# Five weight tiles of the second MoE are kept with a stationary operand's words 2, 4, 6, 8 and 12 words apart

## The chip, the cores and the metric

The kernel runs on one core of a Trainium2 chip. The metric is the device time of one execution in microseconds (us), the median of several runs. One execution was also recorded by the hardware profiler; every row below comes from that record.

## The reference

Inputs are q, k, v and a complex decay per channel (batch 4, 8 heads, 768 steps, 48 channels). A linear-attention recurrence gives 3072 tokens of 384 values, and two feed-forward blocks follow:

```python
x = attn_out.transpose(0, 2, 1, 3).reshape(3072, 384)
h = x @ w_in                                   # 384 -> 2048
x = (h * np.clip(h + 3, 0, 6) / 6) @ w_out     # 2048 -> 384
a, b = x @ w1, x @ w2                          # 384 -> 1024 each
out = ((a * b) @ w3) @ w_out2                  # 1024 -> 1024 -> 384
```

All weights arrive as float64 and are turned into float32 on the chip.

## The kernel before

Precision. A weight or activation is split into a high word (fp32r, rounded by a ScalarE copy) and a low word (fp32r, what VectorE's subtraction leaves). A product of two split operands is three matmuls: high by high, high by low, low by high (`mm3`, L742 to L744). Each matmul has its own stationary load of 128 columns on 128 partitions.

Stages. Until about 586 us attention and the first MoE run interleaved. Then w3 and w_out2 are folded into one 1024x384 matrix (`fold`, L1041 to L1043, up to 620 us). From 620 us to the end the second MoE runs: six blocks of 512 tokens (`two`), and in each block eight slices i of 128 hidden channels. For a slice, `b1` makes x @ w1 and then x @ w2: nine matmuls each (three 128-row pieces kk of the 384 inputs, three products each), with the weight as the stationary operand and 512 tokens as the moving one. ScalarE copies the first result out of PSUM, VectorE multiplies it with the second, and the product is split into `gh` and `gl`. Two slices later `b2` multiplies it with the folded matrix: four token groups of three matmuls, `gh` or `gl` stationary and 384 columns moving (L1104 to L1106).

Weight tiles. Slice i uses columns from group g = i // 2 of w1 and w2: tiles ("1", g) and ("2", g), each 128 partitions by 384 x 256 / 128 = 768 words. A tile is loaded and turned into float32 by `decode` and split by `split` (L764 to L770) into a buffer w of shape [128, 2, 768], tag "W": 768 high words, then 768 low words, each ordered (kk, half i, column). So the 128 words of one stationary operand lie side by side. Three of the eight tiles, ("1", 0), ("2", 0) and ("1", 1), are split elsewhere (`PLACES`) into freed buffers of other names (`ar`, `Kc`, `k`, `q`, `Ks`, `xf`); the other five live in "W". In the profile the second MoE's matmuls and loads named `x<-W` with no second name are just these five; those with a second name are the other three.

Order. A planner (`Plan`) writes the order of each engine's instructions in advance, from estimated durations and due times. Buffers of one tag are handed on when their last reader is done.

Of the kernel before, what the change touches and what calls it, by code (L numbers as in the profile page):

```python
# [7 lines left out]
F32 = mybir.dt.float32  # L8
# [5 lines left out]
AF = mybir.ActivationFunctionType  # L14
ALU = mybir.AluOpType
# [9 lines left out]
EXP_SET, TRIG_SET = "natural_log_exp_and_others", "trig_and_small"  # L25

PLACES = {("o", 0): ("u", "u"), ("o", 1): ("u", "cs"), ("o", 2): ("s1", "s1"), ("o", 3): ("ai", "ai"), ("1", 0): ("ar", "Kc"), ("2", 0): ("k", "q"), ("1", 1): ("Ks", "xf")}
BUFS = {'u': 3, 'ai': 2, 's1': 2, 'ce': 1}


# [226 lines left out]
def c_act(n, psum=False):  # L257
    return n / 1200.0 + (0.05 if psum else 0.095)


def c_tt(n):
    return n / 960.0 + 0.07
# [10 lines left out]
def c_mm(n):  # L273
    return n / 2308.0 + 0.009
# [145 lines left out]
def main_kernel(tc, q, k, v, a_re, a_im, w_in, w_out, w1, w2, w3, w_out2, consts, qT, kT, arT, aiT, vT, wiT, woT, w1T, w2T, w3T, wo2T, out, blocks=(2, 2, 4, 4, 4, 4, 4)):  # L420
# [8 lines left out]
    KD, KF, KI = DM // 128, DFF // 128, DF2 // 128  # L429
# [15 lines left out]
    with tc.tile_pool(name="keep", bufs=1) as kp:  # L445
      c5_ = kp.tile([128, 2, 128], F32, name="c2")
      flag = kp.tile([1, 1], I32, name="flag")
      with ctx:
# [4 lines left out]
        def SB(tag, shape, n=1, dt=F32, free=0, key=None):  # L453
            return P.buf(tag, lambda: sb.tile(shape, dt, tag=tag, name=tag, bufs=P.slots[tag]), n, free, key)

        def WB(shape):

            return SB("W", [128, 2] + shape, NW, F32R)

        def part(w, i, shape):  # L460
            return w()[:, i].rearrange("p (a b) -> p a b", a=shape[0])

        def PS(tag, shape, n=1, free=0):
            return P.buf("ps" + tag, lambda: ps.tile(shape, F32, tag=tag, name=tag, bufs=P.slots["ps" + tag]), n, free)
# [28 lines left out]
        def ACT(dur, fn, r, w, **kw):  # L493
            return P.add("ACT", dur, fn, r, w, **kw)

        def DVE(dur, fn, r, w, **kw):
            return P.add("DVE", dur, fn, r, w, **kw)

        def PE(dur, fn, r, w, **kw):
            return P.add("PE", dur, fn, r, w, **kw)  # L500
# [4 lines left out]
        def A(o, i, f, scale=1.0, bias=0.0, **kw):  # L505
            act.activation(out=o, in_=i, func=f, scale=scale, bias=bias, **kw)  # L506

        def TT(o, i0, i1, op):
            dve.tensor_tensor(out=o, in0=i0, in1=i1, op=op)  # L509
# [10 lines left out]
        def cut(t_, shape):  # L520

            if list(t_.shape) == list(shape):
                return t_
            names = "abc"[:len(shape) - 1]
            size = 1
            for x in shape[1:]:
                size *= x
            s_ = " ".join(names)
            return t_.rearrange("p %s -> p (%s)" % (s_, s_))[:, :size].rearrange("p (%s) -> p %s" % (s_, s_), **dict(zip(names, shape[1:])))
# [13 lines left out]
        def group(gi):  # L543
# [7 lines left out]
            def nb(name, shape=None, n=1, tag=None, full=None):  # L551
                shape = shape or [128, KD, w]
                full = full or shape[:-1] + [shape[-1] * GT // C] if name != "ys" else [128, 4, GT, 128]
                tag = tag or name
                return P.buf(tag, lambda: cut(sb.tile(full, F32, tag=tag, name=tag, bufs=P.slots[tag]), shape), BUFS.get(tag, n))
            ar, ai, kk, qq = (nb(x) for x in ("ar", "ai", "k", "q"))
# [111 lines left out]
        def chunk(u, c_, Kc, KT, QT, ys, mt):  # L668
# [4 lines left out]
            def nb(name, shape=None, n=1, tag=None):  # L673
                return SB(tag or name, shape, BUFS.get(tag or name, n))
            vb = vt[u % 2]
# [65 lines left out]
        def mm3(o, wh, wl, xh, xl, start, stop, **kw):  # L741
            pe.matmul(o, wh, xh, start=start, stop=False, **kw)  # L742
            pe.matmul(o, wh, xl, start=False, stop=False, **kw)  # L743
            pe.matmul(o, wl, xh, start=False, stop=stop, **kw)  # L744

        def load64(src, shape, free, after=()):

            n = shape[0] * shape[1]
            raw = SB("W", [128, 768], NW, U64, free, "raw")
            DMA(lambda e_: e_.dma_start(out=raw()[:, :n].rearrange("p (a b) -> p a b", a=shape[0]), in_=src), after, [raw], n * 1024)  # L750
            return raw, lambda i: raw()[:, :n].bitcast(I32).rearrange("p (n two) -> p n two", two=2)[:, :, i]
# [10 lines left out]
            DVE(c_tt(n), lambda: dve.scalar_tensor_tensor(out=ov().bitcast(I32), in0=words(1), scalar=-0x80000000, in1=words(0), op0=ALU.bitwise_and, op1=ALU.bitwise_or), [lo_], [dst])  # L762
            return lo_

        def split(raw, f):

            w = WB([768])
            ACT(c_act(768), lambda: A(w()[:, 0], f(), AF.Copy), [raw], [w])
            DVE(c_tt(768), lambda: TT(w()[:, 1], f(), w()[:, 0].bitcast(F32), ALU.subtract), [raw, w], [w], part=True)
            return w  # L770

        def packed(raw, n):
            return lambda: raw()[:, :n].bitcast(F32).rearrange("p (two n) -> p two n", two=2)[:, 0, :]

        def pieces(src, i):
            a = KD if src is not woT and src is not wo2T else 2
            return src[i].rearrange("p (a b) -> p a b", a=a), (a, 768 // a)
# [5 lines left out]
        def decode(src, i, after=()):  # L783
            n_ = len(taken_up)
            after = list(after) + ([ready0] if n_ >= EARLY else []) + ([taken_up[n_ - AHEAD]] if n_ >= AHEAD else [])
            src, shape = pieces(src, i)
            raw, words = load64(src, shape, 2, after)
            f = packed(raw, 768)
            taken_up.append(to32(raw, words, 768, raw, f, n_ in EASED))
            return raw, shape  # L790
# [158 lines left out]
        for js in [range(FIRST)] + [[j] for j in range(FIRST, len(blk))]:  # L949
# [18 lines left out]
            for j in js:  # L968
                n = blk[j][1]
# [5 lines left out]
        def half(w, p, i):  # L975

            bufs, shape = w
            if type(bufs) is list:
                t_ = bufs[i]()[:, p]
                return t_.rearrange("p (a b) -> p a b", a=KD) if shape[0] == KD else t_  # L980
            t_ = part(bufs, p, shape)
            return t_[:, :, i * 128:i * 128 + 128] if shape[0] == KD else t_[:, i]

        def of(w, i):
            return w[0][i] if type(w[0]) is list else w[0]

        def later(nm, src, g):
            tags = PLACES.get((nm, g))
            after = [seen[23]]
            if tags is None:  # L990
                raw, shape = decode(src, g, after)
                return split(raw, packed(raw, 768)), shape
            src, shape = pieces(src, g)
            raw, words = load64(src, shape, 1, after)
            f = packed(raw, 768)
            to32(raw, words, 768, raw, f)
            ws = []
            for i, tag in enumerate(tags):
                w = SB(tag, [128, 2, 384], 1, F32R)
                fv = lambda i=i: (f().rearrange("p (a b) -> p a b", a=KD)[:, :, i * 128:i * 128 + 128] if shape[0] == KD else f()[:, i * DM:i * DM + DM])  # L1000
                wv = lambda j, w=w: (w()[:, j].rearrange("p (a b) -> p a b", a=KD) if shape[0] == KD else w()[:, j])
                ACT(c_act(384), lambda fv=fv, wv=wv: A(wv(0), fv(), AF.Copy), [raw], [w])
                DVE(c_tt(384), lambda fv=fv, wv=wv: TT(wv(1), fv(), wv(0).bitcast(F32), ALU.subtract), [raw, w], [w], part=True)
                ws.append(w)
            return ws, shape
# [68 lines left out]
        def b1(j, i, xs):  # L1074
            n = two[j][1] * 128
            pr = []
            for nm in ("1", "2"):
                p_ = PS("x", [128, 512], 5)
                w = wq[nm, i // 2]

                def mm(p_=p_, w=w):
                    wh, wl = half(w, 0, i % 2), half(w, 1, i % 2)
                    for kk in range(KD):
                        mm3(p_()[:, :n], wh[:, kk], wl[:, kk], xs[kk]()[:, 0, :n], xs[kk]()[:, 1, :n], kk == 0, kk == KD - 1)
                PE(9 * c_mm(n), mm, [of(w, i % 2)] + list(xs), [p_, bseq], pin=pins["a", j, i])
                pr.append(p_)
            c = i % 3
            a = SB("r", [128, 512], 2)
            ACT(c_act(n, True), lambda: A(a()[:, :n], pr[0]()[:, :n], AF.Copy), [pr[0]], [a], boost=MB)
            DVE(c_tt(n), lambda: TT(a()[:, :n], a()[:, :n], pr[1]()[:, :n], ALU.mult), [pr[1]], [a], boost=MB)  # L1090
            gh, gl = SB(("u", "u", "s1")[c], [128, 512], 2, F32R), SB(("ai", "ai", "s1")[c], [128, 512], 2, F32R)
            ACT(c_act(n), lambda: A(gh()[:, :n], a()[:, :n], AF.Copy), [a], [gh], boost=MB)
            DVE(c_tt(n), lambda: TT(gl()[:, :n], a()[:, :n], gh()[:, :n].bitcast(F32), ALU.subtract), [a, gh], [gl], boost=MB)
            return gh, gl
# [15 lines left out]
        for j, (a, n) in enumerate(two):  # L1110
            P.bias = -60
            xs = [SB("W", [128, 2, 512], NW, F32R, 2, "xs") for _ in range(KD)]
# [101 lines left out]
```

## Time and profile before

| | |
|---|---|
| median of 3 runs | 928.56 us (926.35 to 928.78) |
| the profiled execution | 927.13 us |
| its span, first to last instruction | 924.9 us |
| TensorE busy | 881.3 us, 95% |
| stationary loads (PEld) busy | 759.0 us, 82% |
| VectorE busy | 585.4 us, 63% |
| ScalarE busy | 508.8 us, 55% |

The span is what the instructions took; the 2.2 us beside it are start and end. Busy shares are averages over stages with different limits. Matmuls are pipelined, so a matmul's record is longer than the distance to the next one; the distance between starts is what it costs. Stationary loads are recorded apart (PEld) and overlap with the matmul before them.

### The profile page before, as it was taken

The page shows a single profiled execution, that of the slowest core. Times are in us where ns is not written, and L with a number is a line of the kernel's source. Part 1 is how long each engine was busy: PE and PEld are TensorE (multiplying, and loading weights), DVE is VectorE, ACT ScalarE, POOL GpSimd, SP SyncE. Part 2 cuts the span into 40 slices and gives each one's busy share as a digit, 9 for nine tenths or more (in the row PEclk, how much of TensorE's full clock was granted, in tenths as well). Part 3 has the DMA queues.
Part 4 walks back from the last instruction along what each step waited for, and adds up shares of the span by engine and source line. Part 5 has one row for each costly group of instructions (what it writes and reads, how often), then busy time and mean ns, then how long its engine had stood idle before and what let it go on. Part 6 is the DMA issues. An engine that isn't in the chain of part 4 may idle for free.

```text
span 924.9 us, 13311 instructions
## 1 busy us (share of the span) xinstructions
PE 881.3 (95%) x5194; PEld 759.0 (82%) x5194; DVE 585.4 (63%) x913; ACT 508.8 (55%) x816; POOL 0.2 (0%) x4
## 2 busy tenths in 40 slices
PE   0689999999999999999999999999999999999997
PEld 0478989888888888878888888998888888888886
DVE  6999999889998787869454699652223223222221
ACT  7999888978887567656423576442222222222221
POOL 0000000000000000000000000000000000000000
PEclk9999999999999999999999999999999999999999
DMA  7895736367581645365424666230100101010001
GB/s 266 213 238 168 198 109 168 95 130 173 157 203 47 165 132 149 80 146 170 94 47 131 195 238 235 93 94 21 34 35 7 62 1 46 1 35 0 16 20 38
DMA packets 55991, 102.88 MB, mean 111 GB/s; under 512 B 6384, under 2 KB 34160, under 8 KB 55920
## 3 DMA queue, kind: packets, MB, share of 16 engines
q1 hardware_dynamic: 55920, 101.94, 39.0%
q8 instruction: 43, 0.70, 0.3%
q14 instruction: 28, 0.23, 0.1%
HBM read 64.62 MB, written 13.63 MB: 85 GB/s over the span
## 4 chain that ended last, share of the span: by engine, by line
PE 75%; DVE 12%; ACT 8%; DMA 3%; issue 1%; SPq 1%; ACTq 0%; DVEq 0%
PE x L742 12%; PE x L743 12%; PE x L744 12%; PE m L742 5%; PE m L743 5%; PE m L744 5%; PE x L693 4%; PE m L1106 3%; PE m L1104 3%; PE m L1105 3%; ACT u L506 2%; ACT W L506 2%; PE x L705 2%; DVE gl L509 1%; PE x L710 1%
## 5 line engine op out<-in xcount | busy, mean ns | idle before, releaser
L506 ACT ACTIVATE r<-x 128x512 f32<-128x512 f32 (+1 forms) x144 | 82.2, 572 | 152.7 <-PE x L744 130.1
L509 DVE TENSOR_TENSOR r<-r,x 128x512 f32<-128x512 f32 x48 | 33.0, 688 | 178.8 <-PE x L744 178.8
L742 PE MATMUL m<-gh,W 128*128 128x512 f32 (+1 forms) x288 | 110.1, 382 | 0.5 <-ACT gh L506 0.5
L743 PE MATMUL m<-gl,W 128*128 128x512 f32 (+1 forms) x288 | 107.7, 374 | 0.9 <-DVE gl L509 0.7
L744 PE MATMUL m<-gh,W 128*128 128x512 f32 (+1 forms) x288 | 107.2, 372 | 0.0
L506 ACT ACTIVATE gh<-r 128x512 fp32r<-128x512 f32 (+1 forms) x96 | 56.7, 593 | 72.9 <-PE m L744 69.3
L742 PE MATMUL x<-xh,W 128*128 128x512 f32 x240 | 96.3, 401 | 0.0
L743 PE MATMUL x<-xl,W 128*128 128x512 f32 x240 | 93.7, 390 | 0.0
L744 PE MATMUL x<-xh,W 128*128 128x512 f32 x240 | 93.6, 390 | 0.0
L509 DVE TENSOR_TENSOR gl<-r,gh 128x512 fp32r<-128x512 f32 (+1 forms) x96 | 61.9, 645 | 43.9 <-ACT gh L506 42.5
L742 PE MATMUL x<-W 128*128 128x512 f32 (+1 forms) x228 | 84.5, 371 | 0.0
L744 PE MATMUL x<-W 128*128 128x512 f32 (+1 forms) x228 | 84.1, 369 | 0.0
L743 PE MATMUL x<-W 128*128 128x512 f32 (+1 forms) x228 | 84.0, 368 | 0.0
L880 DVE SCALAR_TENSOR_TENSOR r<-r,x 128x512 f32<-128x512 f32 (+1 forms) x96 | 61.2, 639 | 13.1 <-ACT r L506 12.7
L506 ACT ACTIVATE W<-W 128x768 f32<-128x768 f32 (+3 forms) x78 | 64.7, 852 | 5.3 <-DMA W<-in_w3T_dram 2.7
L743 PEld LDWEIGHTS m<-gl,W 128*128 128x128 f32 x288 | 54.2, 188 | 11.0 <-DVE gl L509 2.4
L742 PEld LDWEIGHTS m<-gh,W 128*128 128x128 f32 x288 | 54.2, 188 | 11.0 <-issue 0.9
L744 PEld LDWEIGHTS m<-gh,W 128*128 128x128 f32 x288 | 54.2, 188 | 9.6
L506 ACT ACTIVATE u<-r 128x512 fp32r<-128x512 f32 x36 | 22.7, 632 | 63.6 <-DVE r L509 63.6
L742 PEld LDWEIGHTS x<-xh,W 128*128 128x128 f32 x240 | 45.1, 188 | 10.2 <-issue 0.9
L744 PEld LDWEIGHTS x<-xh,W 128*128 128x128 f32 x240 | 45.0, 188 | 9.8
L743 PEld LDWEIGHTS x<-xl,W 128*128 128x128 f32 x240 | 45.1, 188 | 8.4
(216 smaller groups left out, 1911.3 us busy)
## 6 DMA issues: line engine op xcount, KB each, us to landing
KT<-Kc SPq DMA_DIRECT2D x72, 129.0 KB, 3.6
QT<-cs SPq DMA_DIRECT2D x72, 128.0 KB, 4.5
W<-in_w3T_dram SPq DMA_DIRECT2D x16, 512.0 KB, 4.4
v<-in_vT_dram SPq DMA_DIRECT2D x24, 256.0 KB, 2.7
W<-in_wiT_dram SPq DMA_DIRECT2D x8, 768.0 KB, 7.3
W<-in_woT_dram SPq DMA_DIRECT2D x8, 768.0 KB, 7.5
ar<-in_arT_dram SPq DMA_DIRECT2D x12, 384.0 KB, 3.4
ai<-in_aiT_dram SPq DMA_DIRECT2D x12, 384.0 KB, 3.4
```

Of the source, the lines that this page charges most:

```text
L506: act.activation(out=o, in_=i, func=f, scale=scale, bias=bias, **kw)
L509: dve.tensor_tensor(out=o, in0=i0, in1=i1, op=op)
L693: pe.matmul(p_()[:, i, :], KT()[:, 4 * g + i, tok], QT()[:, 4 * g + i, tok])
L705: pe.matmul(py()[64 * j:64 * j + 64, p, :], vb.ap[:, h, :], Pm[h // 4]()[:, h % 4, :], start=True, stop=first, tile_position=(0, 64 * j), ...
L710: pe.matmul(py()[64 * j:64 * j + 64, p, :], Ap.ap[:, h, :], QT()[:, h, tok], start=False, stop=True, tile_position=(0, 64 * j), skip_group ...
L742: pe.matmul(o, wh, xh, start=start, stop=False, **kw)
L743: pe.matmul(o, wh, xl, start=False, stop=False, **kw)
L744: pe.matmul(o, wl, xh, start=False, stop=stop, **kw)
L880: DVE(c_tt(n), lambda: dve.scalar_tensor_tensor(out=r()[:, :n], in0=r()[:, :n], scalar=6.0, in1=h()[:, :n], op0=ALU.min, op1=ALU.mult), [h ...
L1104: pe.matmul(o, gh()[:, a], Wb()[:, 0, i % 2], start=(i == 0), stop=False)
L1105: pe.matmul(o, gh()[:, a], Wb()[:, 1, i % 2], start=False, stop=False)
L1106: pe.matmul(o, gl()[:, a], Wb()[:, 0, i % 2], start=False, stop=(i == KI - 1))
```

## The change

The five tiles that live in "W" get other orders of their 1536 words. `LAID` names for each the distance between neighbouring words of one stationary operand (one kk, one half i, high or low): ("2", 1) 2 words, ("1", 2) 4, ("2", 2) 6, ("2", 3) 8 and ("1", 3) 12. For 2 words, high and low alternate; for 4, the halves i and high/low are interleaved; for 6, the three kk and the halves; for 12, all of these; for 8, kk 0 and 1 are interleaved with everything else, and kk 2 lies behind them with a distance of 4 words. `split` writes the same words with the same engines to the new places, in one instruction each, except that the tile with 8 words needs two on each engine (512 and 256 words). `half` hands `b1` the strided views. The values, the loads' number, the matmuls, the buffers and the planner's costs are as before.

```diff
+LAID = {("2", 1): 2, ("1", 2): 4, ("2", 2): 6, ("1", 3): 12, ("2", 3): 8}
-        def split(raw, f):
+        def split(raw, f, kind=None):
             w = WB([768])
-            ACT(c_act(768), lambda: A(w()[:, 0], f(), AF.Copy), [raw], [w])
-            DVE(c_tt(768), lambda: TT(w()[:, 1], f(), w()[:, 0].bitcast(F32), ALU.subtract), [raw, w], [w], part=True)
+            if kind is None:
...
+            src = lambda: f().rearrange("p (k i c) -> p k i c", k=KD, i=2)
+            def put(fn):
+                for k0, k1 in laid(w, kind, 0)[1]:
+                    fn(laid(w, kind, 0)[0](k0, k1), laid(w, kind, 1)[0](k0, k1), src()[:, k0:k1])
+            ACT(c_act(768), lambda: put(lambda h, l, x: A(h, x, AF.Copy)), [raw], [w])
+            DVE(c_tt(768), lambda: put(lambda h, l, x: TT(l, x, h.bitcast(F32), ALU.subtract)), [raw, w], [w], part=True)
             return w
+        def laid(w, kind, q):
+            x = lambda: w().rearrange("p a b -> p (a b)")
+            whole = ((0, KD),)
+            if kind == 2:
+                return lambda a, b: x().rearrange("p (k i c q) -> p q k i c", k=KD, i=2, q=2)[:, q, a:b], whole
+            if kind == 4:
+                return lambda a, b: x().rearrange("p (k c i q) -> p q k i c", k=KD, i=2, q=2)[:, q, a:b], whole
+            if kind == 6:
+                return lambda a, b: x().rearrange("p (q c k i) -> p q k i c", k=KD, i=2, q=2)[:, q, a:b], whole
+            if kind == 12:
+                return lambda a, b: x().rearrange("p (c k i q) -> p q k i c", k=KD, i=2, q=2)[:, q, a:b], whole
+            return lambda a, b: (x()[:, :1024].rearrange("p (c k i q) -> p q k i c", k=2, i=2, q=2)[:, q] if a == 0 else
+                                 x()[:, 1024:].rearrange("p (k c i q) -> p q k i c", k=1, i=2, q=2)[:, q]), ((0, 2), (2, 3))
...
+            if type(shape[0]) is tuple:
+                get, cuts = laid(bufs, shape[1], p)
+                return [get(a, b)[:, k, i] for a, b in cuts for k in range(b - a)]
...
-                return split(raw, packed(raw, 768)), shape
+                kind = LAID.get((nm, g))
+                return split(raw, packed(raw, 768), kind), (shape if kind is None else (shape, kind))
...
-                        mm3(p_()[:, :n], wh[:, kk], wl[:, kk], xs[kk]()[:, 0, :n], xs[kk]()[:, 1, :n], kk == 0, kk == KD - 1)
+                        mm3(p_()[:, :n], at_k(wh, kk), at_k(wl, kk), xs[kk]()[:, 0, :n], xs[kk]()[:, 1, :n], kk == 0, kk == KD - 1)
```

## Rows read from the trace of the kernel before

**Rows 1.** The page: the granted TensorE clock in 40 slices.
```profile
PEclk9999999999999999999999999999999999999999
```

**Rows 2.** The chain that ended last, 620 to 924.9 us, shares by line.
```profile
by line: PE x L743 21.7%; PE x L744 21.7%; PE x L742 21.5%; PE m L1106 8.3%; PE m L1104 8.3%; PE m L1105 8.3%; PE x L1106 2.7%; PE x L1105 2.7%; PE x L1104 2.7%; DVE xl L1134 0.2%; PE m L1042 0.1%; PE m L1043 0.1%; issue 0.0%
```

**Rows 3.** Windows, block 1: us; busy PE, PEld, DVE, ACT, POOL; clock; DMA.
```profile
683.20:733.00 49.80, 49.80 (x241) 43.84 (x240) 13.76 (x22) 12.30 (x21) 0.00 (x0) 1.00 0.10 32
```

**Rows 4.** Groups by shape, 620 to 924.9 us: loads of the five tiles.
```profile
L742 PEld LDWEIGHTS x<-W 128*128 128x128 f32 x180 | 33.8, 188 | 6.6
L743 PEld LDWEIGHTS x<-W 128*128 128x128 f32 x180 | 33.8, 188 | 6.7
L744 PEld LDWEIGHTS x<-W 128*128 128x128 f32 x180 | 33.8, 188 | 7.1
```

**Rows 5.** Timeline, second MoE: nine x2 matmuls, twelve of b2, the next load.
```profile
655.33 0.39 PE L742 MATMUL x<-W 128*128 128x512 f32 x1
655.34 0.19 PEld L743 LDWEIGHTS x<-W 128*128 128x128 f32 x1
...
657.37 0.33 PE L1104 MATMUL m<-W,u 128*128 128x384 f32 x1
...
659.31 0.19 PEld L742 LDWEIGHTS x<-W 128*128 128x128 f32 x1
659.48 0.39 PE L742 MATMUL x<-W 128*128 128x512 f32 x1
```

**Rows 6.** Timeline, first MoE with 256 moving columns.
```profile
126.39 0.28 PE L742 MATMUL x<-W 128*128 128x256 f32 x1
...
127.47 0.28 PE L742 MATMUL m<-gh,W 128*128 128x256 f32 x1
```

**Rows 7.** Timeline: loads where TensorE comes from another kind of work.
```profile
496.93 0.19 PEld L742 LDWEIGHTS x<-xh,W 128*128 128x128 f32 x1
496.95 0.48 PE L742 MATMUL x<-xh,W 128*128 128x512 f32 x1
497.04 0.19 PEld L743 LDWEIGHTS x<-xl,W 128*128 128x128 f32 x1
```

**Rows 8.** Groups by shape, whole span: loads of 64 columns.
```profile
L705 PEld LDWEIGHTS x<-P,v 128*64 128x64 f32 x368 | 21.6, 136 | 7.1 <-issue 4.6 <-DVE P L509 0.5 <-DVE ai L587 0.4
```

**Rows 9.** Groups by shape, ScalarE: spaced and unspaced operands.
```profile
L506 ACT ACTIVATE W<-W 128x768 f32<-128x768 f32 x28 | 25.7, 924 | 0.8 <-DMA W<-in_w1T_dram 0.5 <-DMA W<-in_wo2T_dram 0.3
L506 ACT ACTIVATE Ks<-x 128x384 f32<-128x384 f32 x40 | 18.2, 484 | 4.9 <-PE x L684 4.8
L506 ACT ACTIVATE W<-W 128x768 fp32r<-128x768 f32 x21 | 17.6, 848 | 1.8 <-DVE W L509 0.9 <-PE m L1043 0.9
L506 ACT ACTIVATE ut<-x 128x384 f32<-128x384 f32 x20 | 9.8, 488 | 5.3 <-PE x L722 5.3
```

**Rows 10.** Groups by shape, VectorE: spaced and unspaced operands, and shorter ones.
```profile
L761 DVE SCALAR_TENSOR_TENSOR W<-W 128x768 int32<-128x768 int32 x28 | 26.9, 961 | 0.7 <-ACT W L506 0.4
L509 DVE TENSOR_TENSOR W<-W 128x768 fp32r<-128x768 f32 x21 | 19.7, 955 | 1.2 <-ACT W L506 1.1
L509 DVE TENSOR_TENSOR gl<-r,gh 128x512 fp32r<-128x512 f32 x80 | 55.2, 690 | 42.2 <-ACT gh L506 41.0 <-PE x L744 0.7
L509 DVE TENSOR_TENSOR gl<-r,gh 128x256 fp32r<-128x256 f32 x16 | 6.7, 420 | 1.6 <-ACT gh L506 1.6
```

**Rows 11.** Timeline: the last splits and what follows them.
```profile
619.06 2.83 DVE L509 TENSOR_TENSOR W<-W 128x768 fp32r<-128x768 f32 x3 [0.75 <-ACT W L506]
...
625.78 0.69 DVE L509 TENSOR_TENSOR ai<-r,u 128x512 fp32r<-128x512 f32 x1 [0.70 <-ACT u L506]
```

**Rows 12.** Timeline, TensorE: first matmul on the five tiles, first b2 matmul.
```profile
630.42 0.39 PE L742 MATMUL x<-W 128*128 128x512 f32 x1
...
632.47 0.33 PE L1104 MATMUL m<-W,u 128*128 128x384 f32 x1
```

More of the change, by code (lines that the diff above doesn't have):

```diff
@@ L763, in to32 @@
             return lo_
-        def split(raw, f):
+        def split(raw, f, kind=None):
             w = WB([768])
-            ACT(c_act(768), lambda: A(w()[:, 0], f(), AF.Copy), [raw], [w])
-            DVE(c_tt(768), lambda: TT(w()[:, 1], f(), w()[:, 0].bitcast(F32), ALU.subtract), [raw, w], [w], part=True)
-            return w
+            if kind is None:
+                ACT(c_act(768), lambda: A(w()[:, 0], f(), AF.Copy), [raw], [w])
+                DVE(c_tt(768), lambda: TT(w()[:, 1], f(), w()[:, 0].bitcast(F32), ALU.subtract), [raw, w], [w], part=True)
+                return w
+            src = lambda: f().rearrange("p (k i c) -> p k i c", k=KD, i=2)
[4 more added lines that the diff above has]
+            DVE(c_tt(768), lambda: put(lambda h, l, x: TT(l, x, h.bitcast(F32), ALU.subtract)), [raw, w], [w], part=True)
+            return w
+        def laid(w, kind, q):
[11 more added lines that the diff above has]
+                                 x()[:, 1024:].rearrange("p (k c i q) -> p q k i c", k=1, i=2, q=2)[:, q]), ((0, 2), (2, 3))
         def packed(raw, n):
@@ L980, in half, with at_k @@
                 return t_.rearrange("p (a b) -> p a b", a=KD) if shape[0] == KD else t_
+            if type(shape[0]) is tuple:
+                get, cuts = laid(bufs, shape[1], p)
+                return [get(a, b)[:, k, i] for a, b in cuts for k in range(b - a)]
             t_ = part(bufs, p, shape)
             return t_[:, :, i * 128:i * 128 + 128] if shape[0] == KD else t_[:, i]
+        def at_k(w, k):
+            return w[k] if type(w) is list else w[:, k]
         def of(w, i):
```

## The prediction

> **What bounds the kernel now.** I read the page first, then the chain of waits, then windows and groups of the second MoE, and last single instructions. [...] From 620 us to the end the chain of work that ended last is matmuls on TensorE and hardly anything else: the nine lines of mm3 and b2 hold 97.9%, VectorE 0.2% (the last copy out), issue 0.0% [rows 2]. A whole block of 512 tokens takes 49.80 us, in which TensorE is busy for 49.80, while VectorE works 13.76 and ScalarE 12.30 [rows 3]. So in this stage a nanosecond added between two matmuls' starts is added to the end, and what VectorE, ScalarE or a DMA does counts only when a matmul has to wait for it.
>
> The stationary loads are the third thing to look at. Those of the five tiles are 3 x 180 = 540, each recorded at 188 ns [rows 4]. A load starts when the matmul before it starts [rows 5], so it runs under that matmul and costs nothing until it is longer than the distance to the next one. That distance is the room. With 512 moving columns it is (657.37 - 655.33) / 9 = 226.7 ns, with b2's 384 columns (659.48 - 657.37) / 12 = 175.8 ns [rows 5].
>
> How much of the room does a load fill? Not 188 ns: at 256 columns matmuls start every (127.47 - 126.39) / 9 = 120 ns, each with its own load [rows 6], so the record holds a part that overlaps the next load. A load of 64 columns is recorded at 136 ns [rows 8], one of 128 at 188 [rows 4]: 52 / 64 = 0.81 ns a column, 104 ns for 128. Where TensorE comes to a split operand from other work, the second load can only start when the first has been taken over by its matmul, and it starts 0.11 us later [rows 7]. So I take 110 ns from a load's start to its matmul: 104 for the words and 6 for handing over.
>
> **The change part by part.** *Loads.* Each slice uses nine loads of a tile, each tile serves two slices, there are six blocks: 108 loads for a tile. The number of loads, matmuls and DMAs stays; only a load's duration can change. Let it be L from start to its matmul. Of the 432 loads of the four tiles with 4 words or more, 24 come first after b2 (x @ w1 in slices 4 to 7, six blocks) and have 175.8 ns of room, as in [rows 5]; the other 408 have 226.7 ns. The 108 loads with 2 words all belong to x @ w2 and have 226.7 ns. The cost is then 24 x (L - 175.8) + 408 x (L - 226.7), each term only where positive.
>
> No load in this trace has spaced words, so L is bounded. From below: spacing costs nothing. ScalarE's copy of 128x384 out of PSUM with 128 words from one element to the next takes 484 ns, and the same size side by side 488 [rows 9]; VectorE's operation with every second word in and out takes 961 ns, the split side by side 955 [rows 10]. Then the sum is 0. From above: the load walks over all words between its own at the pace of a matmul's moving operand, (226.7 - 120) / 256 = 0.417 ns a word [rows 5, 6]. With 6 ns for handing over, L is 219, 326, 433 and 647 ns for 4, 6, 8 and 12 words. Tile ("1", 2) then costs 12 x 44 ns = 0.5 us; ("2", 2) 108 x 100 = 10.7; ("2", 3) 72 x 206 = 14.9 (its 36 loads of kk 2 have 4 words and fit); ("1", 3) 96 x 420 + 12 x 471 = 45.9. Together 72 us. A gain is excluded, since a shorter load gives no matmul an earlier start.
>
> Which value? The nearest row of an SBUF operand that does get slower is ScalarE's copy with every second word in and out, 924 ns against 848 [rows 9], 9% for one skipped word. Carried on at 9% a skipped word, 12 words make the words' time double, 4 to 8 words 1.27 to 1.63 times. I take the double for all four tiles, as the careful end of that: L = 110 + 104 = 214 ns. It fits under 226.7, so 408 loads stay hidden, and 24 show 214 - 176 = 38 ns each: **0.9 us**. With 2 words, 119 ns: hidden. The cover is thin: the words' time may grow to (226.7 - 110) / 104 + 1 = 2.12 times before all 432 loads show, and from there each further nanosecond of L costs 0.43 us.
>
> [...]
>
> *Splits.* Each of the five is one copy on ScalarE (848 ns) and one subtraction on VectorE (955 ns) [rows 9, 10]. The tile with 8 words needs a second one: 690 + 420 - 955 = 155 ns more on VectorE [rows 10], about as much on ScalarE. If spaced writing is free that is all; if it doubles each, VectorE has 5 x 0.955 + 0.155 = 4.9 us more, ScalarE 4.4. Queued behind the last three on VectorE (they end at 621.9 us) are splits of the folded matrix and of later activations, and then slice 0's product, whose low part ends at 626.47 [rows 11]. The first to wait for these is b2 of slice 0 at 632.47, the first strided load comes at 630.42 [rows 12]. 6.0 us of slack cover 4.9, and TensorE's own matmuls are the cover; I put the splits at nothing. Were the cover gone, the excess would be paid once.
>
> The sum against the profiled execution: 927.13 + 0.9 = 928.0 us. That execution lies 1.4 us under the median of the runs, so for the median it is 928.56 + 0.9 = **929.5 us**.
>
> **The rivals.** (a) *A load grows past its matmul* and TensorE waits for each of 408 loads. It decides from 2.12 times the words' time, and from 2.16 times (L = 230 ns) it is over 2.8 us. For it: the margin is 12.7 ns, and the walking bound passes it in three tiles. Against it: the spaced rows of the other engines cost 9% or less. At 2.5 times (L = 266) it is 24 x 90 + 408 x 39 = 18.2 us, 946.8 us; at three times (318) 24 x 142 + 408 x 91 = 40.7 us, 969 us; at the bound 1001 us. [...]
>
> (b) *The change doesn't lengthen the load at all*: words come one by one at the array's pace wherever they lie. The time stays at 928.6 us. For it: the PSUM copy that costs nothing at 128 words, and 0.81 ns a column, which is slower than the moving operand's 0.417 and so leaves time to fetch. Against it: the 9%. [...]
>
> (c) *The splits are late*: spaced writing at three times makes VectorE 9.7 us later, b2 of slice 0 waits 3.7 us once, 932.3 us. Against it: 961 beside 955 ns.
>
> **How the numbers follow.** About 0.3%, 2.8 us, is what a measurement of this kernel can tell from no change. The forecast (longer, but hidden save 24) 0.34; (b) 0.28; (a) between 2.16 and 2.5 times 0.14; (a) beyond 0.17; (c) 0.02; 0.05 for faster, for what no term holds, such as another pattern of meetings between loads and moving reads. So same is 0.62, slower 0.33, faster 0.05. The range goes from 926, just under the lowest of the three runs (926.35), to 947, rival (a) at 2.5 times: 0.62 + 0.14 + 0.02 + a little of the faster ones, 8 in 10. The likeliest one's own range is 927 to 931.4.
>
> **What would show it.** Loads of the four tiles recorded at 188 + 104, about 292 ns, the 2-word tile's at 188 to 200: doubling right. All at 188: (b). Starts 226.7 ns apart inside a nine on spaced words, and only the first matmul after b2 in slices 4 to 7 some 40 ns later: the forecast. Starts 230 ns or more apart in all of slices 4 to 7 and not in slices 0 to 3: (a), and different distances for 4, 6, 8 and 12 words would tell walking from a fixed price. A gap of TensorE near 632 us: (c). The prediction is wrong if a load's words take over 2.16 times their time now.

## The result, and the profile after

The changed kernel takes 936.33 us (935.00 to 937.78, four runs) against 927.59 us for the kernel before beside it: ratio 1.0099, 95% interval 1.0081 to 1.0117. It is slower by 8.7 us. The range held it; the likeliest case, 929.5 us and no measurable change, did not come. What came is rival (a), at its lower end.

The profiled execution took 936.58 us, its span 934.4. Groups by shape from 620 us on, the loads of the five tiles, the counterpart of [rows 4]:

```profile
L744 PEld LDWEIGHTS x<-W 128*128 128x128 f32 x180 | 54.6, 303 | 1.3
L743 PEld LDWEIGHTS x<-W 128*128 128x128 f32 x180 | 54.2, 301 | 1.5
L745 PEld LDWEIGHTS x<-W 128*128 128x128 f32 x180 | 54.0, 300 | 1.4
```

The same 540 loads are recorded at 301 ns instead of 188. That is a mean over the five tiles: 196 ns at 2 words, 312 at 4, 306 at 6, 365 at 12, and 326 on the tile with 8. The idle time before them (last column), 6.6 to 7.1 us a line in [rows 4], is down to 1.3 to 1.5: the loads have hardly a pause left in these slices. That suggests that they are now the bound, and the experiments below test it. A window over one block, the counterpart of [rows 3], has the same columns:

```profile
668.00:719.26 51.26, 51.26 (x241) 48.10 (x241) 13.78 (x23) 12.28 (x22) 0.00 (x0) 1.00 0.09 31
```

A block takes 51.26 us in place of 49.80, TensorE is still busy without a gap, and VectorE and ScalarE do what they did: 1.46 us in each of six blocks is 8.8 us, the whole loss. Nothing outside the second MoE is needed to explain it.

Timeline of block 1, slices 3, 4 and 6, the first matmul of each nine, and of slice 4 the second too (L743 is the high by high product; L1136 begins b2):

```profile
686.74 0.39 PE L743 MATMUL x<-W,xf 128*128 128x512 f32 x1
...
688.83 0.40 PE L743 MATMUL x<-W 128*128 128x512 f32 x1
...
690.94 0.34 PE L1136 MATMUL m<-W,u 128*128 128x384 f32 x1
...
693.02 0.46 PE L743 MATMUL x<-W 128*128 128x512 f32 x1
693.32 0.40 PE L744 MATMUL x<-W 128*128 128x512 f32 x1
...
695.20 0.40 PE L743 MATMUL x<-W 128*128 128x512 f32 x1
...
697.33 0.34 PE L1136 MATMUL m<-W,s 128*128 128x384 f32 x1
...
705.82 0.48 PE L743 MATMUL x<-W 128*128 128x512 f32 x1
...
708.28 0.41 PE L743 MATMUL x<-W 128*128 128x512 f32 x1
...
710.46 0.34 PE L1136 MATMUL m<-W,u 128*128 128x384 f32 x1
```

The differences of starts are what a nine takes. The kernel before has, on the tiles of slice 4 (x @ w1, then x @ w2, then b2):

```profile
659.48 0.39 PE L742 MATMUL x<-W 128*128 128x512 f32 x1
659.71 0.40 PE L743 MATMUL x<-W 128*128 128x512 f32 x1
...
661.56 0.39 PE L742 MATMUL x<-W 128*128 128x512 f32 x1
...
663.60 0.33 PE L1104 MATMUL m<-W,s 128*128 128x384 f32 x1
```

So x @ w1 took 2.08 us and x @ w2 2.04, and slices 5 to 7 (and x @ w2 of 2 and 3) are alike. Against these, as means over the six blocks, worked out before rounding:

| tile | words apart | nine matmuls, us | more | times 12 slices, us |
|---|---|---|---|---|
| ("2", 1) | 2 | 2.11 | 0.07 | 0.9 |
| ("1", 2) | 4 | 2.18 | 0.10 | 1.2 |
| ("2", 2) | 6 | 2.13 | 0.08 | 1.0 |
| ("1", 3) | 12 | 2.47 | 0.39 | 4.6 |
| ("2", 3) | 8 | 2.17 | 0.13 | 1.6 |

The sum is 9.3 us; b2's twelve matmuls behind a spaced tile take 2.08 to 2.10 us instead of 2.11 [rows 5], which gives 0.6 of it back. Half of the loss is the one tile with 12 words. In x @ w1 the first load, which runs beside b2, costs most: from the first matmul to the second it is 295 ns with 4 words (693.02 to 693.32) and 320 with 12, in place of 229 (659.48 to 659.71).

### The profile page after: what moved, and what is told of

Read it like the earlier page. It is cut to its first block, busy times and chain, and to the rows that moved or that the text cites. A ratio compares the mean times of both kernels' runs of the same rounds, so it can differ in the third digit from the quotient of the medians.

```text
span 934.4 us, 13313 instructions
## 1 busy us (share of the span) xinstructions
PE 890.7 (95%) x5194; PEld 785.2 (84%) x5194; DVE 587.9 (63%) x914; ACT 511.7 (55%) x817; POOL 0.2 (0%) x4
## 4 chain that ended last, share of the span: by engine, by line
PE 79%; ACT 10%; DVE 7%; DMA 1%; issue 1%; SPq 1%; ACTq 0%; DVEq 0%
PE x L743 13%; PE x L745 13%; PE x L744 13%; PE m L743 5%; PE m L744 5%; PE m L745 5%; PE x L694 4%; ACT u L507 3%; PE m L1136 3%; PE m L1138 3%; PE m L1137 3%; ACT W L507 3%; ACT L1176 2%; PE x L706 2%; PE x L711 1%; PE m L1073 1%
## 5 line engine op out<-in xcount | busy, mean ns | idle before, releaser
L743 PE MATMUL m<-gh,W 128*128 128x512 f32 (+1 forms) x288 | 110.1, 382 | 0.5 <-ACT gh L507 0.5
L743 PE MATMUL x<-xh,W 128*128 128x512 f32 x240 | 96.3, 401 | 0.0
L743 PE MATMUL x<-W 128*128 128x512 f32 (+1 forms) x228 | 89.3, 392 | 0.0
L744 PE MATMUL x<-W 128*128 128x512 f32 (+1 forms) x228 | 86.4, 379 | 0.0
L745 PE MATMUL x<-W 128*128 128x512 f32 (+1 forms) x228 | 86.4, 379 | 0.0
L507 ACT ACTIVATE W<-W 128x768 f32<-128x768 f32 (+4 forms) x79 | 68.0, 885 | 5.1 <-DMA W<-in_w3T_dram 2.4
L905 DVE SCALAR_TENSOR_TENSOR r<-r,x 128x512 f32<-128x512 f32 (+1 forms) x96 | 60.9, 637 | 13.2 <-ACT r L507 12.7
L744 PEld LDWEIGHTS x<-W 128*128 128x128 f32 x228 | 63.7, 279 | 1.4
L743 PEld LDWEIGHTS x<-W 128*128 128x128 f32 x228 | 63.3, 278 | 1.8
L745 PEld LDWEIGHTS x<-W 128*128 128x128 f32 x228 | 63.1, 277 | 1.4
L743 PEld LDWEIGHTS m<-gh,W 128*128 128x128 f32 x288 | 54.2, 188 | 11.0 <-issue 0.9
```

The lines of the kernel that those rows point to most:

```text
L905: DVE(c_tt(n), lambda: dve.scalar_tensor_tensor(out=r()[:, :n], in0=r()[:, :n], scalar=6.0, in1=h()[:, :n], op0=ALU.min, op1=ALU.mult), [h ...
```

## The experiments

Two theories of what stretches a nine. A: a spaced load simply takes longer than its matmul, whatever the matmul does. B: the load takes the predicted 214 ns, and the matmul's reading of its moving operand is slowed by the load's. And two questions beside them: do the splits take part, and does a price belong to the distance or to the tile's place?

### Loads without splits, splits without loads

`loads_only` writes the tiles as before and reads them at the spaced places; `splits_only` does the reverse.

```diff
-                return split(raw, packed(raw, 768), kind), (shape if kind is None else (shape, kind))
+                return split(raw, packed(raw, 768)), (shape if kind is None else (shape, kind))      # loads_only
+                return split(raw, packed(raw, 768), kind), shape                                      # splits_only
```

> The changed kernel's spaced loads alone: the splits write as in the kernel before, and b1 reads the spaced places (so its weights are words in another order). Theory, all of the loss is in the loads: slower by 0.9 to 1.0%, as the whole change, slices as in its trace (2.18 and 2.13 us for nine matmuls at 4 and 6 words, 2.46 and 2.17 at 12 and 8). Rival, part of it is in the late splits: less than 0.9%.

> The changed kernel's spaced splits alone: they write to the new places, and b1 reads side by side as before (again another order of the weights). Theory, the splits are covered: within 0.2% of the kernel before, ScalarE and VectorE some 3 us busier in all, no gap of TensorE near 630 us. Rival, the splits cost: slower by up to 0.1 to 0.4%.

Loads alone: 936.36 us, ratio 1.0099 (1.0083 to 1.0114), the whole loss to the last digit. Splits alone: 927.96 us, 1.0003 (0.9994 to 1.0012), nothing. The splits did get slower. Groups by shape in `splits_only`, ScalarE from 596 to 640 us:

```profile
L507 ACT ACTIVATE W<-W 128x768 fp32r<-128x768 f32 x4 | 5.7, 1472 | 0.1
L507 ACT ACTIVATE W<-W 128x512 fp32r<-128x512 f32 x1 | 1.3, 1274 | 0.3 <-DVE W L510 0.3
```

A split is 848 ns with its words side by side [rows 9]; the four here average 1472, the one with two-word steps among them. In the changed kernel, which writes to the same places, the one with two-word steps takes 913 ns by itself, the other three 1584 to 1710. VectorE's part for 512 words at 8 words distance takes 1158 ns in the changed kernel, against 690 [rows 10]. In the changed kernel slice 0's low part ends at 628.60 + 0.69 = 629.3 us, and b2 of slice 0 starts at 633.37: the slack of 6.0 us is down to 4.1, and nobody waits.

### Fewer moving columns beside the same loads

`n256` and `n384` cut b1's moving operand, so that the loads cannot hide and their own time shows. The diff is that of `n256`; `n384` has 384 and t % 3, and in both the copy, product and split behind b1 are cut alike.

```diff
-mm3(p_()[:, :n], at_k(wh, kk), at_k(wl, kk), xs[kk]()[:, 0, :n], xs[kk]()[:, 1, :n], ...)
+mm3(p_()[:, :256], at_k(wh, kk), at_k(wl, kk), xs[kk]()[:, 0, :256], xs[kk]()[:, 1, :256], ...)
-                    a = slice(t * 128, t * 128 + 128)
+                    a = slice(t % 2 * 128, t % 2 * 128 + 128)
```

> The changed kernel, with b1's matmuls and the four operations behind them on 256 moving columns in place of 512 (the second half of each block's tokens is not computed; b2 takes the first two token groups twice). At 256 columns an unspaced load left matmuls 120 ns apart. Theory A, the load itself is the bound: the spaced tiles keep the distances that they have at 512 columns, about 236 ns for 4 and 6 words, 243 for 8, 267 for 12, and the 2-word tile falls to about 120 to 125. Theory B, the load takes a fixed 214 ns and the matmul's reading of its moving operand is slowed by the load's reading: 4, 6, 8 and 12 words all come to 214 to 220 ns, and the 2-word tile to 120 plus half of the 8 ns that it has at 512. Unspaced tiles: 120 in both.

> The changed kernel with 384 moving columns in b1 (the last quarter of each block's tokens is not computed). Unspaced: about 173 to 176 ns between matmuls. Theory A: again 236 for 4 and 6 words, 243 for 8, 267 for 12, and the 2-word tile at 173 to 180. Theory B: 214 to 220 for 4 to 12 words, since the matmul with its slowing (176 plus some 7) is then shorter than the load.

Timeline of `n256`, the first matmuls of nines in block 1 (`xf` unspaced, then 2 words, b2, 4 words, 6 words, b2; then 12 and 8 words):

```profile
672.08 0.28 PE L743 MATMUL x<-W,xf 128*128 128x256 f32 x1
...
673.15 0.28 PE L743 MATMUL x<-W 128*128 128x256 f32 x1
...
674.23 0.34 PE L1136 MATMUL m<-W,u 128*128 128x384 f32 x1
...
676.31 0.34 PE L743 MATMUL x<-W 128*128 128x256 f32 x1
...
678.35 0.39 PE L743 MATMUL x<-W 128*128 128x256 f32 x1
...
680.40 0.34 PE L1136 MATMUL m<-W,s 128*128 128x384 f32 x1
...
688.74 0.37 PE L743 MATMUL x<-W 128*128 128x256 f32 x1
...
691.09 0.41 PE L743 MATMUL x<-W 128*128 128x256 f32 x1
...
693.24 0.34 PE L1136 MATMUL m<-W,u 128*128 128x384 f32 x1
```

Unspaced and 2 words: 1.07 and 1.08 us, 120 ns a matmul. 4 and 6 words: 2.04 and 2.05 us, 227 and 228 ns on average. 12 and 8 words: 2.35 and 2.15, 261 and 239. Half the moving columns, and the spaced tiles keep almost all of their distance: the load is the bound, and B with its 214 to 220 falls. At 384 columns the nines of 2, 4, 6, 12 and 8 words take 1.56, 2.11, 2.07, 2.40 and 2.16 us, where unspaced ones take 1.56. A holds, but not to the nanosecond: for 6 words its 236 at 512 columns is 228 at 256. So the load's own interval is 228 ns there, and something more is added beside 512 columns.

### Other distances, and other places

`steps` places the operands by number, so that any distance s fits (the rest of a tile lies 12 - s apart, and a split takes six instructions on each engine); `steps_n256` does it with 256 columns; `swap` and `only12` keep the original layouts.

```diff
-LAID = {("2", 1): 2, ("1", 2): 4, ("2", 2): 6, ("1", 3): 12, ("2", 3): 8}
+LAID = {("2", 1): 9, ("1", 2): 11, ("2", 2): 7, ("1", 3): 10, ("2", 3): 12}   # steps, steps_n256
+            if n < s:                                                          # operand n of 12
+                return x[:, :128 * s].rearrange("p (c s) -> p s c", s=s)[:, n]
+            return x[:, 128 * s:].rearrange("p (c s) -> p s c", s=12 - s)[:, n - s]
+LAID = {("2", 1): 12, ("1", 2): 2, ("2", 2): 8, ("1", 3): 6, ("2", 3): 4}     # swap
+LAID = {("1", 3): 12}                                                         # only12
```

> The changed kernel with other distances, 512 moving columns: tile (2,1) 9 words, (1,2) 11, (2,2) 7, (1,3) 10, (2,3) 12; operands that find no room at that distance lie 12 minus it apart (3, 1, 5, 2 words). Theory A with a load that grows with the stretch it walks from about 7 words on (243 ns at 8, 267 at 12, so 6 ns a word): 237 at 7, 249 at 9, 255 at 10, 261 at 11, 267 at 12 in its new place; 1 word 227, 2 words 235, 3 and 5 words 235 to 236. Rival, the price belongs to the tile's place (x @ w1 in slices 6 and 7) and not to the distance: 267 at (1,3) with 10 words, 243 at (2,3) with 12. Rival, the price depends on the distance's divisibility and not its size: odd distances (7, 9, 11) at 236 or less, 10 and 12 more.

> The same distances (9, 11, 7, 10, 12 words, the rest of a tile at 3, 1, 5, 2) with 256 moving columns in b1 (second half of the tokens not computed). Theory A: the same distances between matmuls as at 512 where the load is longer than 227 there, and the load's own time for the short ones: 1 word 120, 2 words 120 to 125, 3 words between 120 and 214, 5 words 214 to 236. Theory B: 214 to 220 from 4 words on, whatever the distance.

Timeline of `steps_n256`, slices 2 and 3 of block 1. In slice 2 eight matmuls have operands 9 words apart and the ninth 3 (the low words of kk 2 found no room at 9); in slice 3 six have 9 words and three have 3. L1128 begins b2:

```profile
670.08 0.40 PE L743 MATMUL x<-W 128*128 128x256 f32 x1
...
672.00 0.34 PE L745 MATMUL x<-W 128*128 128x256 f32 x1
672.17 0.34 PE L1128 MATMUL m<-W,u 128*128 128x384 f32 x1
...
675.33 0.41 PE L743 MATMUL x<-W 128*128 128x256 f32 x1
...
676.77 0.34 PE L743 MATMUL x<-W 128*128 128x256 f32 x1
...
677.30 0.33 PE L1128 MATMUL m<-W,u 128*128 128x384 f32 x1
```

The distance behind a matmul goes with that matmul's own load. 9 words: 1.92 / 8 = 240 ns and 1.44 / 6 = 240. 3 words: 0.17 us once and 0.53 / 3 = 177 ns, half way between 120 and 234. Read in the same way from all blocks of this run and `n256`, a load's interval is

| words apart | 2 | 3 | 4 | 5 | 6 | 7 | 8 | 9 | 10 | 11 | 12 |
|---|---|---|---|---|---|---|---|---|---|---|---|
| ns | under 120 | 176 | 234 | 227 | 228 | 233 | 242 | 240 | 236 | 251 | 268 |

(In slices where x @ w1 is spaced the first load is left out: it starts beside b2, and in `n256` the distance behind it is 0.17 to 0.21 us. The value at 8 is that of the six loads with 8 words.) So the time grows up to 4 words, stays between 227 and 242 ns up to 10, and grows again at 11 and 12. The growth in proportion from 7 words that I expected, 249, 255 and 261 ns at 9, 10 and 11, isn't there: at 512 columns (`steps`) 9 words come to 243 ns, 10 to 242 and 11 to 255. Divisibility by 2 doesn't sort them either: 5 and 7 pay as 4 and 6 (227 and 233 ns beside 234 and 228), and 11 pays more than 10 (251 beside 236). Why 11 and 12 pay more, and what makes the smaller steps between 4 and 10, stays open. `steps` itself took 940.24 us in its one run; its 12-word tile, now in x @ w2, takes 2.41 us in nine, 267 ns.

> The same five distances on other tiles: (2,1) 12 words, (1,2) 2, (2,2) 8, (1,3) 6, (2,3) 4. Theory, the price belongs to the distance: the loss stays near 0.9 to 1.0%, nine matmuls at 12 words now take about 267 x 9 = 2.40 us in slices 2 and 3 (they come behind 512 columns, so without the longer first load), and slices 6 and 7 fall to 2.18 and 2.13. Rival, it belongs to the place: slices 6 and 7 keep 2.46.

> Of the change only the tile with 12 words. From the changed kernel's trace its nine matmuls take 2.46 to 2.47 us against 2.08, two slices a block, six blocks: 12 x 0.385 = 4.6 us, a ratio of about 1.005, so more than half of the loss of 8.7 us. Rival, every spaced tile costs about alike, a fifth each: 1.7 us, 1.002.

`swap`: 935.41 us, 1.0081 (1.0067 to 1.0095). The 12-word tile's nine in slice 2, first matmul and the b2 behind it:

```profile
682.53 0.44 PE L743 MATMUL x<-W 128*128 128x512 f32 x1
...
684.93 0.34 PE L1136 MATMUL m<-W,u 128*128 128x384 f32 x1
```

2.40 us, as expected, and slices 6 and 7 fall to 2.18 and 2.11: the price of 12 words belongs to the distance. The loss, 0.8%, lies a little under the expected 0.9 to 1.0: the 12-word tile has no first load beside b2 here, and the 2-word tile, now in x @ w1, takes 2.09 us, 0.01 more than unspaced, where in x @ w2 it was 0.07. `only12`: 932.44 us, 1.0058 (1.0044 to 1.0072), so more than half of the loss with one of five tiles. It is 5.1 us, and not all of it lies on the tile: the unspaced nines of x @ w2 behind it grew too, from 2.04 to 2.08 or 2.09 us.

### The doubled load alone, and the last four columns

`all4` gives all five tiles 4 words, the clean case of the prediction's "double"; `n480` and `n508` cut b1's columns, as `n384` does, so that the matmul is just under the load's interval, and to just under 512.

```diff
+LAID = {("2", 1): 4, ("1", 2): 4, ("2", 2): 4, ("1", 3): 4, ("2", 3): 4}       # all4
```

> All five tiles with 4 words. What the prediction's step would make of it: every load doubled, 24 + 12 loads behind b2 show, under 1.5 us, ratio 1.000 to 1.002. Theory A with the load's interval at 236 ns beside 512 columns: nine matmuls 2.18 at x @ w1 (from 2.08) and 2.12 at x @ w2 (from 2.04), so a block 4 x 0.10 + 6 x 0.08 = 0.88 us, less about 0.1 in b2: 4.7 us in six blocks, ratio 1.005.

> The changed kernel with 480 moving columns in b1 (the last 32 tokens of each block are not computed; b2 takes its fourth token group from the first). Unspaced matmuls should start 480 x 0.417 + 13.3 = 213.3 ns apart. At 256, 384 and 512 columns the 6-word tile's nine took 2.05, 2.07 and 2.12 us, the 2-word tile's nine 1.07, 1.56 and 2.11 where the unspaced had 1.07, 1.56 and 2.04. Theory D, what is above the load's own 227 ns, and the 2-word tile's 8 ns, come only where the load's interval (or the matmul's) meets 512 full columns: 2.07 to 2.08 us for 6 words, 1.92 (213 ns) for 2 words. Theory C, each moving column read beside a spaced load costs a little: 2.10 to 2.11 for 6 words, and 1.97 to 1.98 for 2 words.

> The changed kernel with 508 moving columns in b1 (the last 4 tokens of each block not computed, b2's fourth token group taken from the first). Unspaced by the line of 256 and 384 columns: 225.0 ns, nine in 2.02 to 2.03 us. At 512 x @ w1's nine take 2.08 where x @ w2's take 2.04, at 384 both 1.56. Theory D (a matmul of the full 512 columns is what is special): both 2.03 here, 2 words 2.03, 6 words at the load's own 2.07. Theory C: as at 512 less 0.02, so 2.06 and 2.02 for the unspaced, 2.09 and 2.10 to 2.11 for 2 and 6 words.

`all4`: 932.26 us, 1.0054 (1.0040 to 1.0067). The prediction's step, 0.000 to 0.002, is refuted by itself: a doubled load is not hidden by 512 columns. (Tile ("2", 1) never comes first behind b2, so the 12 loads added there don't exist; the step as it stands has 24, 0.9 us.) Timeline of `all4`, slice 4 of block 1 (x @ w1, x @ w2, b2), nines of 2.18 and 2.11 us:

```profile
691.97 0.46 PE L743 MATMUL x<-W 128*128 128x512 f32 x1
...
694.15 0.40 PE L743 MATMUL x<-W 128*128 128x512 f32 x1
...
696.26 0.34 PE L1136 MATMUL m<-W,s 128*128 128x384 f32 x1
```

At 480 columns 6 words take 2.08 us in nine (231 ns) and 2 words 1.95 beside 1.94 unspaced; at 508 columns 6 words take 2.12 (236). Timeline of `n508`, slice 3 of block 0, unspaced, then 2 words, then b2:

```profile
634.97 0.39 PE L743 MATMUL x<-W,xf 128*128 128x508 f32 x1
...
637.02 0.39 PE L743 MATMUL x<-W 128*128 128x508 f32 x1
...
639.07 0.34 PE L1136 MATMUL m<-W,u 128*128 128x384 f32 x1
```

2.05 us for both. Theory D is right for the 2-word tile: its 0.07 us at 512 columns is gone with the last four columns, and so is the difference between x @ w1 and x @ w2. For the longer loads neither theory fits: 228, 230, 231, 236 and 236 ns for 6 words at 256, 384, 480, 508 and 512 columns. With 6 words the extra comes where the matmul's own interval (2.05 / 9 = 228 ns at 508) is as long as the load's 228. The 4-word tile does not follow this: from its second matmul on it has 234, 234, 240, 235 and 236 ns at the same widths. So what a load and a matmul of nearly equal length cost each other is not shown beyond these numbers.

## Why the prediction was right and wrong, point by point

**The bound and where the cost would lie: right.** The second MoE is a row of matmuls without a gap, the loss is 1.46 us in each block, and `loads_only` has all of it.

**The doubling: right, for 4 to 7 words.** The trace shows it in a single load. Timeline of the changed kernel, slice 4's first spaced load, starting with b2's last matmul (other engines' lines left out):

```profile
641.58 0.34 PE L1138 MATMUL x<-W,ai 128*128 128x384 f32 x1
641.59 0.31 PEld L743 LDWEIGHTS x<-W 128*128 128x128 f32 x1
641.76 0.46 PE L743 MATMUL x<-W 128*128 128x512 f32 x1
641.80 0.34 PEld L744 LDWEIGHTS x<-W 128*128 128x128 f32 x1
642.05 0.40 PE L744 MATMUL x<-W 128*128 128x512 f32 x1
642.06 0.31 PEld L745 LDWEIGHTS x<-W 128*128 128x128 f32 x1
```

The next load starts 0.21 us later, which read as in [rows 7] is the predicted L of 214 ns. The one behind it comes 0.26 us later, and the rest of the nine 0.23 to 0.24 us apart. With 256 columns the intervals at 2, 3 and 4 words are under 120, 176 and 234 ns (`n256`, `steps_n256`), and 251 and 268 at 11 and 12. What in the chip sets these prices, no run shows.

**The room: this step failed.** The prediction gave the load 214 of 226.7 ns and a margin of 12.7. It took 6 ns for handing over from one pair of loads after a pause, which start 0.11 us apart [rows 7]; that the second waits for such a handing over was a reading, and no run shows the 6 ns by itself. In a row of loads the interval is 227 to 234 ns at 4 to 7 words: words doubled, 2 x 104 ns by the estimate from [rows 4, 8], and some 20 to 26 ns more, which no run takes apart; the matmuls themselves show 13 ns above their columns, 120 for 256 columns x 0.417 = 106.7 on the line through 256 and 512 columns [rows 5, 6], and 384 columns lie on it with 173 (`n384`, 1.56 / 9). The room was misread too: 226.7 ns is a nine of x @ w2, and x @ w1's nines took 231 a matmul (2.08 / 9) in the kernel before already. So the margin was nothing in x @ w2 and at most a few ns in x @ w1. The 24 first loads were expected to show 38 ns each and showed 66 with 4 words and 91 with 12. Of the 408 that were put at nothing, those with 4 words showed 4 ns each, with 6 words 9, those of the 8-word tile some 15 and those with 12 words 37. `all4` puts the step at 5 us where it had 0.9. The prediction's own sign of being wrong, over 2.16 times the words' time, came.

**The longest step: mis-sized.** ScalarE's 9% for one skipped word, carried on, gave 12 words a doubling and no more. A 12-word load takes 268 ns, 34 more than a 4-word one with 234 (`n256`), and 4.6 of the 9.3 us are that tile's. ScalarE's row was no measure for a load at all: between 2 and 4 words the load's interval goes from under 120 ns to 234, and from 4 to 10 words it stays between 227 and 242. The walking bound (647 ns) was far off as well.

**2 words: nearly right.** Its loads are recorded at 196 ns, and at 256, 384, 480 and 508 columns its nines take what unspaced ones take, within 0.01 us (1.08, 1.56, 1.95 and 2.05 us beside 1.07, 1.56, 1.94 and 2.05). At 512 the tile costs 0.9 us, a term that the sum didn't have.

**The splits: right.** Spaced writing does slow them from 4 words on, by 1.5 to 2 times (in the changed kernel ScalarE takes 1584 to 1710 ns for 768 words against 848, VectorE 626 for 256 words against 420 [rows 9, 10]), and the cover held: `splits_only` has 1.0003.

**The rivals.** (a), at 0.14 and 0.17, is what happened: the four tiles' distances of 236 to 267 ns lie at 2.2 to 2.5 times the words' time by the prediction's own formula, for which it gave 2.8 to 18.2 us. The stated range held the time because it was drawn to take this rival in, and not through the forecast's own case. (b), at 0.28, was far off: the same 128 words cost by where they lie, up to 120 ns at 1 and 2 words apart, 234 at 4 and 268 at 12 (`n256`). (c) did not come: `splits_only` has 1.0003.

## What to carry to other kernels

A stationary load that is hidden has a room, the distance to the next matmul (here 227 or 231 ns with 512 columns, 176 with b2's 384), and a price that depended here on how its words lie: 128 fp32r words up to 2 apart fitted under 120 ns, 3 apart took 176, 4 to 12 apart 227 to 268 (`n256`, `steps_n256`). Before calling a longer load hidden, take its interval from a row of loads and not from a first one (0.23 to 0.24 us against 0.21), take the room from each kind of matmul that hides it, and count a tie as a loss: with 6 words and 508 columns load and matmul have 228 ns each, and the nine took 236 a matmul. To measure a load, shorten the matmul that hides it: with 256 moving columns each distance from 3 words on could be read directly.

## What was not expected

Distances of 11 and 12 words cost more than 4 to 10 (251 and 268 ns against 227 to 242). A matmul with 512 moving columns can take 227 or 231 ns on unspaced operands of the same shape (2.04 and 2.08 us for nine), and up to 235 beside a load whose words lie 2 apart (2.11); with 508 columns all three take 227 to 229. The unspaced nines of x @ w2 in `only12` went from 227 to 231 or 232 ns behind a spaced tile, so part of what the table puts on the x @ w2 tiles may be of this kind; it is not shown how much. ScalarE's and VectorE's splits at 8 words distance take 1274 (`splits_only`) and 1158 ns (the changed kernel) for 512 words, instead of 629 (ScalarE's `gh` in the kernel before) and 690 [rows 10], though VectorE's two-word steps took 961 ns where side by side took 955 [rows 10]; VectorE also reads the high words at that distance.
